# When three pieces of side work are handed out in a fused attention and gated-MLP kernel: the pause of a row-sum ring, one exponential, one total

## The chip, the cores and the metric

The kernel runs on one core of a Trainium2 chip. The metric is the device time of one execution in microseconds. Before the change it is 770.04 us (median of three runs, 769.9 to 770.56). The profiled execution has a span of 768.1 us and a mean granted TensorE clock of 0.999 of full speed, so the clock plays no part here.

The engines are named as follows. TensorE (PE) does the matmuls and PEld its weight loads; VectorE (DVE) and ScalarE (ACT) do the elementwise work; GpSimd (POOL) some sums and some transfers; SyncE (SP) issues most of the DMA transfers. Each engine works through its own queue in order, and waits for the others by semaphores.

## The reference

The sequence has 2048 rows of width 1024 in bf16. The first half is attention in which each position sees 8 positions, two apart, in 32 heads of 32; the second half is a gated MLP with 3584 hidden columns and no nonlinearity. Layernorm stands before both, and each half adds to its input.

```
def _A_ref(x, wqkv, wo):                      # H = 32, Dh = 32, W = 8, dil = 2
    qkv = (x @ wqkv).reshape(B, S, 3, H, Dh)  # then q, k, v as (B, H, S, Dh)
    idx = arange(S)[:, None] - (arange(W) * dil)[None, :]
    kg, vg = k[:, :, idx], v[:, :, idx]       # idx < 0 is masked
    logits = einsum("bhsd,bhswd->bhsw", q, kg) * Dh ** -0.5
    o = einsum("bhsw,bhswd->bhsd", softmax(logits), vg)
    return o.transpose(0, 2, 1, 3).reshape(B, S, D) @ wo

def _B_ref(x, w_gate, w_up, w_down):
    return ((x @ w_gate) * (x @ w_up)) @ w_down

h  = x + _A_ref(_layernorm(x), wqkv, wo)
h2 = h + _B_ref(_layernorm(h), w_gate, w_up, w_down)
```

## The kernel before

**Tiles and stages.** The rows go in four chunks of 512 (`TC`). A matmul has 128 x 128 weights and 512 moving columns, and fills one PSUM bank; a group of eight accumulates over the depth of 1024. All PSUM tiles come from one pool of eight banks. The stages in order of time, from the profile's chain of waits: the q, k, v projections to 188 us (with the output projection `wo` of chunk 0 from 155 to 169); the MLP's gate and up products of chunk 0 (`ffn1_first`, from 188 to 298, with `wo` of chunk 1 from 257 to 271); those of chunk 1 (`ffn1_second`, from 298 to 396); `wo` of chunk 2 (`wo_adds`); the down product of chunks 0 and 1 to 474; `wo` of chunk 3; the rest of that down product to 510; gate, up and down of chunks 2 and 3 to the end.

**Fewer products, scaled to f16.** Some of the large products are done as seven products of half size and not eight, on sums and differences of quarter matrices (`dprod` for the down product). For these, operands are turned into f16 with a power of two as scale, taken from the sum of absolute values. A `Scale` collects that: `add` sums the absolute values of a piece on ScalarE into one column of `l1` (L369, an activation with an accumulator, 1.90 us for 128 x 2048); `rows` adds up the columns on VectorE (L373, L374); `total` spreads the sum over the partitions by a matmul with ones (L379), and makes the factors from it on VectorE (L381 to L388). `scale_d` is that of `w_down`.

**The ring.** Of `w_down`, twelve pieces are summed when they are loaded for use (`abs_blocks`), and nine are loaded for their sum alone. That is `abs_down` (L678): one buffer of the weight pool (`wpool`, seven buffers) holds two pieces in turn, each loaded by a DMA that ScalarE issues (L688) and summed by ScalarE (L369). The summed piece is then overwritten by the load of the piece after next.

**The planner.** `Background` deals out side work between the matmul groups while the program is written. Each piece of side work is a Python generator. After every group, `bg.step(GROUP_US)` adds 1.73 us of credit and lets generators run up to their next `yield`; a number is the VectorE time to charge, and `("later", t)` says not to come back before t us of the planner's time. So a `yield` decides where in each engine's queue the next instructions stand, before the chip has seen anything. `abs_down` asks for `6.0 * GROUP_US` between pieces.

**Side work around the change.** Attention 2 and 3 are such generators: VectorE forms the logits (L546 to L556), takes their maximum off (L562 to L567), ScalarE does the exponential in two halves (L570), VectorE sums (L573) and multiplies with v (L594 on). So is `Norm2.finish`, the second layernorm of chunk 1 on ScalarE after `wo_1`: row sums and squares (L279, L637, L638), the normalized rows (L304), and their transposition by DMA (L632) for `ffn1_second`.

**Chunk 1 of the MLP.** `ffn1_second` runs seven blocks of four gate and four up groups. Each group gets a bank, and ScalarE casts it into one of three parts of a small ring in SBUF (L783). VectorE multiplies gate and up (L766), SyncE stores the product to `hd1` in DRAM (L769), and when that has landed the part of the ring can be written again. ScalarE also sums absolute values here, of the products and of weights (L369). SyncE's queue holds these stores and the loads of the weights (L172) in the order in which the planner met them; a load is put there when a buffer of the seven has been given back (`retire`, `pump`).

**The down product.** In the loop over q at L1228 VectorE converts `a21` and `a22` (L1084), with `scale_d.rows()` between them, and TensorE runs `scale_d.total` in the third round, ahead of the rest of that round's work. The factors from it release the conversions of the weights and their differences `t` (L1096), which TensorE takes from 447 us on.

Of the kernel before, what the change touches and what calls it, by code (L numbers as in the profile page):

```python
# [78 lines left out]
def kernel(  # L79
# [47 lines left out]
    def f16(ap):  # L127
        return ap.bitcast(F16)
# [37 lines left out]
    def pump(limit=None, wt=None):  # L166
        state["limit"] = limit or state["limit"]
        while state["next"] < state["limit"] and state["live"] < 7:
            key, src, n = stream[state["next"]]
            if wt is None:  # L170
                wt = wpool.tile([128, KO, 512], BF, tag="w", name="w_" + "_".join(map(str, key)))
            nc.sync.dma_start(wt[:, 0:n, :], src)  # L172
            wts[key] = wt
            wt = None
            state["next"] += 1
            state["live"] += 1

    def retire(n=1):
        state["live"] -= n
        pump()  # L180
# [22 lines left out]
    def load_x(c, what, eng, after=None):  # L203
        tiles = []
        for t in range(4):
            xt = hp.tile([128, D], BF, tag="h", name=f"{what}{c}_{t}")
            if after is not None and t == 0:
                nc.gpsimd.tensor_copy(xt[:, 0:1], after)
            eng.dma_start(xt[:], x[bass.ds(c * TC + t * 128, 128), :])
            tiles.append(xt)  # L210
        return tiles
# [275 lines left out]
    def mm_group(ps, wt, j, rhs):  # L487
        for ko in range(KO):
            nc.tensor.matmul(ps[:], lhsT=wt[:, ko, bass.ts(j, 128)], rhs=rhs[:, ko, :],  # L489
                             start=(ko == 0), stop=(ko == KO - 1))  # L490
# [44 lines left out]
    def attention(c):  # L535
# [29 lines left out]
        nc.vector.tensor_tensor(mx[:], tr[:, 0], tr[:, 1], ALU.max)  # L565
        for ws in (slice(0, 4), slice(4, 8)):
            nc.vector.tensor_tensor(lg[:, ws], lg[:, ws], mx[:, None, :].to_broadcast((128, W // 2, SUB)), ALU.subtract)  # L567
        yield "later", 4.0 if c == 0 else 1.5
        for ws in (slice(0, 4), slice(4, 8)):
            nc.scalar.activation(lg[:, ws], lg[:, ws], ACTF.Exp, scale=float(DH) ** -0.5)  # L570
        yield 3.5
# [99 lines left out]
    scale_gu, scale_d, scale_h = Scale("gu", 28), Scale("d", 21), Scale("h", 56)  # L671
    scale_h1 = Scale("h1", NF + NP)

    def abs_sum(key, c, b, i, junk):
        wt = wts[key, c, b]
        scale_gu.add((14 if key == "wu" else 0) + 2 * b + i, wt[:, bass.ts(i, 4), :], junk)

    def abs_down():  # L678
        ring = wpool.tile([128, KO, 512], BF, tag="w", name="w_ring")

        def rows_of(p):
            return ring[:, bass.ds(4 * (p % 2), pieces[p].shape[1]), :]

        pieces = [wd_v[:, bass.ts(p, 4), 512:1024] for p in range(7)]
        pieces += [wd_e[0][:, 0:4, 0:512], wd_e[0][:, 4:7, 0:512]]

        def load(p):
            nc.scalar.dma_start(rows_of(p), pieces[p])  # L688

        for p in range(2):  # L690
            load(p)
        yield "later", 12.0
        for p in range(9):
            scale_d.add(p, rows_of(p), rows_of(p))
            if p + 2 < 9:
                load(p + 2)
            yield "later", 6.0 * GROUP_US
        retire()

    def abs_blocks(tiles):  # L700
# [10 lines left out]
    def ffn1_first(lnT, at):  # L711
        hT, late = [], []
        junk = lnTp.tile([128, 4, 512], BF, tag="lnT", name="junk_g")

        def finish():
            gs, us = late.pop()
            nc.vector.tensor_tensor(gs[:], gs[:], us[:], ALU.mult)
            bg.spend(0.36)
            hT.append(gs)

        def sum_h(f):
            if f >= 0:
                scale_h1.add(f, hT[f][:], junk[:, 0, :])

        for b in range(7):
            if b == 2:
                hss[1] = load_x(1, "h", nc.sync)
            for j in range(4):
                if (b, j) in at:
                    at[b, j]()  # L730
                pg = psum.tile([128, TC], F32, tag="mm", name=f"pg0_{b}_{j}")
                mm_group(pg, wts["wg", 0, b], j, lnT)
                gs = t1k.tile([128, TC], BF, tag="t1k", name=f"gs0_{b}_{j}")
                nc.scalar.copy(gs[:], pg[:])
                if late:
                    finish()
                bg.step(GROUP_US)
                pu = psum.tile([128, TC], F32, tag="mm", name=f"pu0_{b}_{j}")
                mm_group(pu, wts["wu", 0, b], j, lnT)
                us = t1k.tile([128, TC], BF, tag="t1k", name=f"us0_{b}_{j}")  # L740
                nc.scalar.copy(us[:], pu[:])
                late.append((gs, us))
                if j % 2 and b not in (4, 5):
                    abs_sum("wg", 0, b, j // 2, junk[:])
                sum_h(len(hT) - 2)
                bg.step(GROUP_US)
            retire(2)
        finish()
        for f in range(NF - 3, NF):
            sum_h(f)  # L750
        return hT

    def ffn1_second(lnT, at):
        ring = [lnTp.tile([128, KO, TC], BF, tag="lnT", name=f"ring{i}") for i in range(2)]
        junk = ring[1][:, 4:8, :]
        late, done = [], []

        def sum_last():
            if done:
                i, g = done.pop()  # L760
                scale_h1.add(NF + i, g, junk[:, 0:2, :])

        def finish():
            i, g, u = late.pop(0)
            sum_last()
            nc.vector.tensor_tensor(g, g, u, ALU.mult)  # L766
            bg.spend(0.62)
            done.append((i, g))
            nc.sync.dma_start(hd1[:, bass.ts(i, 2), :], g)  # L769

        for b in range(7):
            if b == 5:
                hss[2] = load_x(2, "h", nc.sync)
            if b == 6:
                bg.spend(8.0)
            for j in range(4):
                i, k = divmod(4 * b + j, 2)
                part = ring[i % 3 // 2][:, bass.ts(i % 3 % 2, 4), :]
                g, u = part[:, 0:2, :], part[:, 2:4, :]
                for what, dst in (("wg", g), ("wu", u)):  # L780
                    ps = psum.tile([128, TC], F32, tag="mm", name=f"p{what}1_{b}_{j}")
                    mm_group(ps, wts[what, 1, b], j, lnT)
                    nc.scalar.copy(dst[:, k, :], ps[:])  # L783
                    if what == "wg" and late:
                        finish()
                    if what == "wu":
                        if k:
                            late.append((i, g, u))
                        if j % 2:
                            abs_sum("wu", 1, b, j // 2, junk)  # L790
                        elif b in (4, 5):
                            abs_sum("wg", 1, b, j // 2, junk)
                    bg.step(GROUP_US)
            retire(2)
            if b in at:
                at[b]()
        finish()
        sum_last()
# [275 lines left out]
    bg.add(sums, bg.now + 10.0, first=True)  # L1074
    hT0 = ffn1_first(lnT2_0, {(5, 0): wo_1})
    bg.finish(norm2[1])
    ffn1_second(norm2[0].lnT, {})
    bg.finish(sums)

    def to_f16(dst, src, sc, eng=nc.vector):  # L1080
        if eng is nc.scalar:
            nc.scalar.activation(dst, src, ACTF.Copy, scale=sc)
        else:
            eng.tensor_scalar(dst, src, sc, None, ALU.mult)  # L1084
# [56 lines left out]
    def cells_of(homes, n=8):  # L1141
        return [t[:, k, :] for t in homes for k in range(n)][0:NP]
# [55 lines left out]
    def s1_half(i):  # L1198
        n = (8, 6)[i]
        s, t = (f16(a[i][:, 0:n, :]) for a in (a21, a22))  # L1200
        nc.vector.tensor_tensor(s, s, t, ALU.add)

    def conv_h1(a, i, eng=nc.vector):
        n = (8, 6)[i]
        to_f16(f16(a[i][:, 0:n, :]), a[i][:, 0:n, :], scale_h1.s, eng)
# [22 lines left out]
    for q in range(4):  # L1228
        dprod(xs[q], q, A11, cells_of(b11, NH), True)
        if q == 0:  # L1230
            conv_h1(a21, 0)
            scale_d.rows()
            conv_h1(a22, 0)
        if q == 1:
            conv_h1(a21, 1, nc.scalar)
        if q == 2:
            scale_d.total(ys[3])
            inv1 = const.tile([128, 1], F32, name="inv_h1d")
            nc.vector.tensor_tensor(inv1[:], scale_h1.inv, scale_d.inv, ALU.mult)
            inv1 = inv1[:]  # L1240
            s1_half(0)
            for i in range(3):
                seed(i)
            conv_h1(a22, 1, nc.scalar)
# [28 lines left out]
    for q in range(4):  # L1273
        ev = psum.tile([128, TC], F32, tag="mm", name=f"ev{q}")
        dprod(ev, q, FS1, fcells(b11), True)
        p = lnp.tile([128, TC], F32, tag="ln", name=f"ep5_{q}")
# [173 lines left out]
    for q in range(4):  # L1450
        dprod(ps_x[q], q, S1, fcells(t1h), True)
        p = lnp.tile([128, TC], F32, tag="ln", name=f"dp5_{q}")
# [60 lines left out]
```

## Time and profile before

| | before |
|---|---|
| time, median of 3 | 770.04 us (769.9 to 770.56) |
| span of the profiled execution | 768.1 us |
| TensorE busy | 761.1 us, 99% |
| VectorE busy | 627.5 us, 82% |
| ScalarE busy | 533.0 us, 69% |
| DMA, mean rate | 190 GB/s |

The page gives the busy time of each engine. A wait is listed as the engine and line that waited, the engine and line that released it, the sum in us, how often, and the longest. A line of the timeline has the start, the length, the engine, the line of the kernel, the operation, out<-in, the shape and the count, and in brackets the idle time before it and who ended it. TensorE's lengths overlap, because matmuls are pipelined: the starts tell the pace. In a table by stage each engine's busy time is followed by its number of instructions, and the last three columns are the granted clock, the DMA share and GB/s.

Where the page puts ScalarE's work of interest: the nine sums of the ring start between 212.3 and 311.5 us; the normalized rows of chunk 1 (L304) at 282.97, 285.20, 287.90 and 291.96; the exponentials of attention 2 at 294.66 and of attention 3 at 384.03.

### The profile page before, as it was taken

The numbers are of one execution on the slowest core, as the hardware profiler recorded it, in microseconds if no ns is written. First come the engines' busy times: TensorE is split into PE (matmuls) and PEld (weight loads), VectorE is DVE, ScalarE is ACT, GpSimd is POOL, SyncE is SP. The second block draws the span as 40 slices with busy tenths as digits, with TensorE's granted clock in tenths as the row PEclk, the third lists the DMA queues.
The fourth block names the chain that finished last, engine by engine and source line by source line (L and its number), as shares of the span: only waits on it lengthen the run. The fifth ranks groups of instructions, "written<-read, shape, count | busy, mean of one in ns | idle before, by whom it ended". The sixth has DMA issues, their size and how long they took to land.

```text
span 768.1 us, 10356 instructions
## 1 busy us (share of the span) xinstructions
PE 761.1 (99%) x3648; PEld 349.3 (45%) x3648; DVE 627.5 (82%) x760; ACT 533.0 (69%) x1012; POOL 144.5 (19%) x155
## 2 busy tenths in 40 slices
PE   8999999999999999999999999999999999999998
PEld 6444444444444444444444444444444444444444
DVE  6789999999999998999999999976554444578862
ACT  4756854556799599975899985846777677788230
POOL 0010000200001000001000002008778777600000
PEclk9999999999999999999999999999999999999999
DMA  8899794967998959779679438684242423830001
GB/s 273 224 236 261 187 285 117 308 180 192 328 347 283 301 193 312 242 248 310 199 242 301 154 109 268 152 201 131 72 109 56 111 81 84 263 121 27 1 28 55
DMA packets 191987, 145.77 MB, mean 190 GB/s; under 512 B 81856, under 2 KB 182080, under 8 KB 189888
## 3 DMA queue, kind: packets, MB, share of 16 engines
q1 hardware_dynamic: 180416, 116.94, 53.5%
q0 software_dynamic: 3728, 22.02, 8.4%
q10 hardware_dynamic: 7792, 6.16, 2.7%
q8 instruction: 28, 0.46, 0.3%
q14 instruction: 23, 0.19, 0.1%
HBM read 111.02 MB, written 27.26 MB: 180 GB/s over the span
## 4 chain that ended last, share of the span: by engine, by line
PE 75%; DVE 14%; ACT 5%; issue 2%; DMA 2%; SPq 0%; ACTq 0%; DVEq 0%
PE ps L489 17%; PE dx L1103 6%; PE pz L843 6%; PE px L843 6%; PE py L843 6%; PE pg L489 6%; PE pu L489 5%; PE wo L661 4%; PE ez L1103 3%; PE pv L843 3%; PE ey L1103 3%; PE dy L1103 3%; DVE prod L546 2%; PE wo L1157 2%; DVE pv L594 2%
## 5 line engine op out<-in xcount | busy, mean ns | idle before, releaser
L489 PE MATMUL ps<-lnT,w_qkv 128*128 128x512 bf16 x608 | 132.1, 379 | 0.0
L489 PEld LDWEIGHTS <-w_qkv 128*128 128x128 bf16 (+1 forms) x608 | 59.3, 98 | 70.9
L546 DVE TENSOR_TENSOR prod<-qD,kD 128x4096 bf16<-128x4096 bf16 (+1 forms) x34 | 72.3, 2158 | 2.9 <-DMA kD<-kd 2.9
L594 DVE TENSOR_TENSOR pv<-vD,at 128x4096 bf16<-128x4096 bf16 x32 | 72.4, 2285 | 0.3
L489 PEld LDWEIGHTS <-w_wg 128*128 128x128 bf16 x448 | 43.8, 98 | 54.1 <-issue 1.3
L843 PEld LDWEIGHTS <-sw 128*128 128x128 f16 x448 | 43.8, 98 | 52.9 <-issue 0.2
L489 PEld LDWEIGHTS <-w_wu 128*128 128x128 bf16 x448 | 43.8, 98 | 52.9
L403 ACT CAST sg<-ps 128x512 bf16<-128x512 f32 x72 | 41.6, 584 | 31.1 <-PE ps L489 26.6
L843 PE MATMUL px<-lnT,ws 128*128 128x512 bf16 x224 | 55.2, 379 | 0.0
L489 PE MATMUL pwg<-lnT,w_wg 128*128 128x512 bf16 x224 | 52.9, 379 | 1.0 <-ACT ring L783 1.0
L489 PE MATMUL pu<-lnT,w_wu 128*128 128x512 bf16 x224 | 52.9, 379 | 0.0
L489 PE MATMUL pg<-lnT,w_wg 128*128 128x512 bf16 x224 | 52.9, 379 | 0.0
L489 PE MATMUL pwu<-lnT,w_wu 128*128 128x512 bf16 x224 | 52.9, 379 | 0.0
L843 PEld LDWEIGHTS <-ws 128*128 128x128 f16 x336 | 32.9, 98 | 39.6
L607 POOL DMA_DIRECT2D od<-oD x4 | 2.2, 542 | 253.3 <-DVE oD L605 253.3
L824 POOL TENSOR_TENSOR sw<-ws 128x512 f16<-128x512 f16 x26 | 30.0, 1153 | 78.8 <-ACT pz L868 47.1
L1103 PEld LDWEIGHTS <-gs 128*128 128x128 f16 (+1 forms) x280 | 27.2, 98 | 34.3 <-issue 1.3
L548 DVE TENSOR_TENSOR prod<-prod 128x4096 bf16<-128x4096 bf16 x16 | 36.6, 2287 | 0.3
L860 ACT COPY py<-px 128x512 f32<-128x512 f32 x28 | 16.0, 570 | 24.5 <-PE px L843 24.5
L827 POOL TENSOR_TENSOR sw<-ws,sw 128x512 f16<-128x512 f16 x26 | 30.6, 1175 | 0.0
L825 POOL TENSOR_TENSOR sw<-sw,ws 128x512 f16<-128x512 f16 x26 | 30.0, 1154 | 2.0
L826 POOL TENSOR_TENSOR sw<-ws 128x512 f16<-128x512 f16 x26 | 30.2, 1161 | 0.0
(371 smaller groups left out, 1577.5 us busy)
## 6 DMA issues: line engine op xcount, KB each, us to landing
w_wg<-in_B_w_gate_dram SPq DMA_DIRECT2D x14, 1024.0 KB, 7.9
w_wu<-in_B_w_up_dram SPq DMA_DIRECT2D x14, 1024.0 KB, 7.7
w_pair<-in_B_w_gate_dram SPq DMA_DIRECT2D x14, 512.0 KB, 4.0
w_pair<-in_B_w_up_dram SPq DMA_DIRECT2D x14, 512.0 KB, 5.3
w_wo<-in_A_wo_dram SPq DMA_DIRECT2D x6, 1024.0 KB, 8.3
w_qkv<-in_A_wqkv_dram SPq DMA_DIRECT2D x5, 1024.0 KB, 9.2
kd<-sg SPq DMA_DIRECT2D x32, 144.0 KB, 4.2
vd<-sg SPq DMA_DIRECT2D x32, 144.0 KB, 3.4
```

The source lines that it names most:

```text
L403: nc.scalar.copy(sg[:, HB:HB + TC], ps[:])
L489: nc.tensor.matmul(ps[:], lhsT=wt[:, ko, bass.ts(j, 128)], rhs=rhs[:, ko, :], start=(ko == 0), stop=(ko == KO - 1))
L546: nc.vector.tensor_tensor(prod[:, j, ds], qD[:, ds], kD[:, ds, o:o + SUB], ALU.mult)
L548: nc.vector.tensor_tensor(prod[:, :, 0:16], prod[:, :, 0:16], prod[:, :, 16:32], ALU.add)
L594: nc.vector.tensor_tensor(pv[:, j], vD[:, :, o:o + SUB], at[:, w, None, :].to_broadcast((128, DH, SUB)), ALU.mult)
L661: nc.tensor.matmul(ps[:], lhsT=oTs[c][:, kk, t, :], rhs=wts["wo", c, hf][:, kk, :], start=(kk == 0), stop=(kk == KO - 1))
L824: eng.tensor_tensor(sw[:, i, 0], a21, a22, ALU.add)
L825: eng.tensor_tensor(sw[:, i, 1], sw[:, i, 0], a11, ALU.subtract)
L826: eng.tensor_tensor(sw[:, i, 2], a11, a21, ALU.subtract)
L827: eng.tensor_tensor(sw[:, i, 3], a12, sw[:, i, 1], ALU.subtract)
L843: nc.tensor.matmul(ps[:], lhsT=lhs[:, ko, :], rhs=rhs[:, ko, :], start=(fresh and ko == 0), stop=(ko == 3), skip_group_check=not fresh)
L1103: nc.tensor.matmul(ps[:, bass.ds(lo, n)], lhsT=lhs[k][:, bass.ts(q, 128)], rhs=rhs[k][:, bass.ds(lo, n)], start=(fresh and k == 0), stop=( ...
```

## The change

Three edits of order. No instruction is added or dropped on any engine, apart from the places where they stand.

1. `abs_down` stops after its fifth piece (p == 4) until the second layernorm of chunk 1 has been written out (`normed`), and goes on in chunk 1. It is meant to leave ScalarE to the layernorm and to attention 2's exponential.
2. Attention 3 hands out its exponential 3.0 us and not 1.5 us of planner's time after its logits: one group later. It is meant to let one more cast go ahead of it.
3. `scale_d.rows()` goes ahead of the conversion of `a21`, so that the total's matmul has its operand earlier.

On ScalarE's queue the first edit moves pieces 5 to 8 of the ring. They stood in chunk 0's blocks 5 and 6 and at the first group of chunk 1; now they stand after the first up group of chunk 1's block 0, after that block's weight sum, in the middle of block 1 and in the middle of block 2. The buffer of the ring is given back later. In SyncE's queue the gate weights of chunk 1's blocks 4, 5 and 6 therefore each move behind the one or two ring stores that followed them. The second edit swaps the two exponentials with one cast (L783, block 5, j 1, gate). The third swaps VectorE's L373 and L374 with one L1084. TensorE's and GpSimd's orders are unchanged.

```diff
@@ attention(c)
-        yield "later", 4.0 if c == 0 else 1.5
+        yield "later", {0: 4.0, 3: 3.0}.get(c, 1.5)
         for ws in (slice(0, 4), slice(4, 8)):
             nc.scalar.activation(lg[:, ws], lg[:, ws], ACTF.Exp, scale=float(DH) ** -0.5)
@@ before abs_down
+    normed = set()
@@ abs_down
             if p + 2 < 9:
                 load(p + 2)
             yield "later", 6.0 * GROUP_US
+            while p == 4 and 1 not in normed:
+                yield "later", 1.0
         retire()
@@ main order
     hT0 = ffn1_first(lnT2_0, {(5, 0): wo_1})
     bg.finish(norm2[1])
+    normed.add(1)
     ffn1_second(norm2[0].lnT, {})
@@ down product, for q in range(4)
         dprod(xs[q], q, A11, cells_of(b11, NH), True)
         if q == 0:
+            scale_d.rows()
             conv_h1(a21, 0)
-            scale_d.rows()
             conv_h1(a22, 0)
```

## The prediction

> **What bounds the kernel now.** I read the page's busy shares first, then who waits for whom on TensorE, then the timelines around each of its waits. TensorE is at work almost throughout, and it waited only three times for as much as 0.3 us after the start-up:
>
> ```profile
> PE 761.1 (99%) x3648; PEld 349.3 (45%) x3648; DVE 627.5 (82%) x760; ACT 533.0 (69%) x1012; POOL 144.5 (19%) x155
> ```
> ```profile
> PE pwg L489 <- ACT ring L783: 1.0, 1, 1.0
> ...
> PE ey L379 <- DVE rowbd L374: 0.3, 1, 0.3
> PE ey L1103 <- DVE t L1096: 0.3, 1, 0.3
> ```
>
> Busy time of pipelined matmuls flatters, so I took start to start: consecutive 512-column matmuls start 0.216 us apart (a group of eight takes 1.73 us), and anything beyond is lost. After the first 20 us the start times show eight such gaps of 0.06 us or more: 1.20 us at 384.6, 0.45 at 419.2, 0.10 at 447.1, 0.43 at 448.7, and 0.12, 0.20, 0.08 and 0.25 at 462, 498, 514 and 717. Their sum, 2.83 us, is all that a change of order can save; more than that would need fewer matmuls.
>
> The largest gap, TensorE's timeline and then ScalarE's:
>
> ```profile
> 381.13 1.89 PE L489 MATMUL pwg<-lnT,w_wg 128*128 128x512 bf16 x8
> 382.86 1.89 PE L489 MATMUL pwu<-lnT,w_wu 128*128 128x512 bf16 x8
> 385.79 1.89 PE L489 MATMUL pwg<-lnT,w_wg 128*128 128x512 bf16 x8 [1.04 <-ACT ring L783]
> ```
> ```profile
> 378.22 1.98 ACT L369 ACTIVATE ring<-w_wg 128x2048 bf16<-128x2048 bf16 x1
> 380.03 0.26 ACT L369 ACTIVATION_READ_ACCUMULATOR ring<-w_wg 128x1 f32 x1
> 384.03 1.23 ACT L570 ACTIVATE lg<-lg 128x512 f32<-128x512 f32 x2 [3.74 <-DVE lg L567]
> 385.17 0.57 ACT L783 CAST ring<-pwg 128x512 bf16<-128x512 f32 x1
> 385.64 0.59 ACT L783 CAST ring<-pwu 128x512 bf16<-128x512 f32 x1
> ```
>
> The reader should see ScalarE's queue stopped for 3.74 us at attention 3's exponential, for logits that VectorE has not finished. The cast behind it is of group (block 5, j 1, gate), whose matmuls ended at 372.5. All eight banks are full, so TensorE stands until that cast returns one. ScalarE was late already: 5.21 us at 362.75 for a store of the ring that landed late, behind weight loads.
>
> VectorE is the next limit. In the table by stage (TensorE, its weight loads, VectorE, ScalarE, GpSimd) it has 13.8 to 13.9 us of every 14 from 298 to 382, of which these two rows are the first:
>
> ```profile
> 298.00:312.00 14.00, 14.00 (x66) 6.37 (x65) 13.92 (x11) 13.12 (x25) 0.00 (x0) 1.00 1.04 316
> 312.00:326.00 14.00, 14.00 (x67) 6.36 (x65) 13.91 (x8) 14.00 (x24) 0.00 (x0) 1.00 0.65 203
> ```
>
> It lost time just before, to a late ScalarE:
>
> ```profile
> 293.71 0.42 DVE L717 TENSOR_TENSOR gs<-gs,us 128x512 bf16<-128x512 bf16 x1 [1.09 <-ACT us L741]
> 295.86 0.69 DVE L573 TENSOR_TENSOR trs<-lg 128x512 f32<-128x512 f32 x1 [1.72 <-ACT lg L570]
> ```
>
> And the second gap, VectorE's order, then TensorE's:
>
> ```profile
> 418.08 1.28 DVE L1084 TENSOR_SCALAR a<-a,sbh 128x4096 f16<-128x4096 bf16 x1
> 419.27 0.17 DVE L373 TENSOR_REDUCE rowd<-l1d 128x1 f32<-128x21 f32 x1
> 419.48 0.16 DVE L374 CAST rowbd<-rowd 128x1 bf16<-128x1 f32 x1
> ```
> ```profile
> 419.69 0.38 PE L379 MATMUL ey<-rowbd,ones 128*128 128x512 bf16 x1 [0.28 <-DVE rowbd L374]
> ```
>
> TensorE was ready at 419.24; the total had to wait for a conversion that nobody needed yet.
>
> **What the Trainium skill says.** "TensorE: Matmul & The Clock Gate", Back-to-back issue gap and the lines before it, gives 216 ns between 512-column matmuls; this trace has 0.216. "PSUM — Partial Sum Buffer", Specifications (TRN2), gives 8 banks, each for one 512-column fp32 output; the trace agrees, as TensorE stopped when the group eight back was not yet cast. "ScalarE: Activation LUTs", What ACT_TABLE_LOAD costs, prices an ACTIVATE with immediates at 186 ns + 0.833 ns a column, 1.89 us for 2048; the ring sums here took 1.90. "DMA: Bandwidth & Descriptors", Queues, rings and completion order, has the issues of one queue on one set of rings, each consumed in order, so that a small store stands behind earlier loads; here the store issued at 352.98, after two 1 MB loads at 345.2 and 345.7, landed only at 362.7.
>
> **Part 1, the ring's pause.** Comparing the order of instructions on each engine, pieces 5 to 8 of the w_down row sum leave ScalarE's queue at 272.07, 289.04, 300.45 and 311.46 and come back between 311 and 338, one each at about block 0 start, block 0 end, block 1 middle, block 2 middle of chunk 1. Each costs 1.90 us (the last 1.49), and where it issues a load 0.5 more with the semaphore; nothing is added or removed.
> Gain: at 272 ScalarE can instead take the third row tile as soon as VectorE's addition ends (272.8), so 274.51 becomes about 272.9: 1.6 us. Piece 6 gives 2.4 more. Attention 2's exponential at 294.66 could then start at 290.7, but its logits end at 292.62 less the 0.82 us that VectorE no longer waits at 280.70: 291.8. So the sums at 295.86 start at about 293.2, and VectorE is 2.66 us ahead. Since it has next to no idle time from 298 to 384, it keeps that.
> Cost: ScalarE's backlog was 10.5 us at 310.5 (the cast of a group whose matmuls ended at 299.98). VectorE's lead shrinks it to 7.9; the four pieces then add 0.9, 2.4, 1.9 and 1.5, against casts and sums that leave ScalarE 2.7 us idle per 14 after 326. I get backlogs of 6.4 at block 1 and about 4 at block 2. TensorE stops only when a backlog passes about 11.5 us (seven groups of 1.73 less the cast): nothing on the path. The ring's buffer is held some 27 us longer, so chunk 1's gate weights of blocks 4, 5 and 6 are issued behind one or two ring stores: at about 330, 342 and 351, needed at 353, 367 and 381. With 8 us to land, hidden. The new order also puts the store at 352.98 ahead of one of the two loads, so the 5.21 us wait at 362.75 should be nearly gone.
>
> **Part 2, the exponential a group later.** One cast now goes ahead of the two activations. The cast of 385.17 runs at about 380 and the bank is free 5 us sooner; the next cast (385.64) inherits the wait. Its bank is needed 1.73 us later, at 386.3, and it ends by 385.8: the 1.20 us are saved even with everything else late, and with part 1's 2.7 us there is slack. VectorE's sums behind the exponential still follow VectorE's own logits at once. Cost nothing, as ScalarE was idle 3.74 us there.
>
> **Part 3, the total first.** The reduce and its cast (0.4 us with their semaphores) pass ahead of a 1.2 us conversion. The last partial sum's accumulator is read at 418.2, so they could end at 418.6, 0.6 us before TensorE comes: 0.45 us saved. Behind them the two conversions start 0.4 us later or less; VectorE's own reading of the total follows TensorE's matmul.
>
> **The later gaps.** The total then lets VectorE go on at about 418.7 and not 420.76, so 2.0 us earlier; TensorE comes 1.75 us earlier to the t factors (1.20 + 0.45 + 0.10). Of the 0.43 us, 0.43 − (2.0 − 1.75) = 0.18 stay. The four small gaps stay; they follow VectorE. Sum: 1.20 + 0.45 + 0.10 + 0.25 = 2.0 us, and 770.04 − 2.0 = 768.0.
>
> **Rivals.**
> A, only the bank gap goes: VectorE does not keep its lead (a ring store or a late cast takes it), and TensorE meets the same waits for the total or the t factors again. 770.04 − 1.2 = 768.8. For it: VectorE is 99% busy from 412 to 440 and 95% from there to 474, so any delay there returns. Against: the order is the same and no wait on it gets later.
> B, no stall is left: 770.04 − 2.83 = 767.2. For it: VectorE 2 us earlier might cover the small gaps too. Against: TensorE gets just as much earlier.
> C, slower: the ring's sums in chunk 1 meet an undiminished backlog. 10.5 + 2.4 + 2.4 = 15.3 us is 3.8 over the 11.5 that eight banks hold, less the 0.45 of part 3: 773.4. For it: ScalarE was 14.0 us busy of 14 from 312 to 326. Against: the same work has left the stretch before.
> D, the stalls move and cancel, say a bank wait of 1 to 2 us at 386 to 390, as ScalarE's casts of block 5 run 11 to 12.5 us late in the trace of before: 769.8.
>
> **How the numbers follow.** Forecast 0.50, A 0.20, B 0.13, D 0.07, C 0.10. The time is 768.0. The range from 766.9 (B and the spread of the runs) to 769.8 (D) leaves out C and a little. Faster by over 0.2% is below 768.5: the forecast and B, 0.62 with a little off for their edges and from A; the same, A and D, 0.27; slower 0.11.
>
> **What would show it.** Right: no TensorE wait for ACT L783 near 384, none for rowbd; the wait before the trs sums at 295 below 1.1 us; ScalarE's wait for a ring store near 362 under 1 us; the first cast of chunk 1 near 308; total span about 766. Wrong: a TensorE wait for a bank between 310 and 345 (C) or at 386 to 390 (D), a wait for w_wg in blocks 4 to 6, or VectorE at the t factors no earlier than before (A).

## Result and profile after

The changed kernel takes 767.78 us (median of six runs, 767.47 to 768.34) against 770.07 for the kernel before on the same chip: 2.3 us less, ratio 0.997 with a 95% interval of 0.9957 to 0.9982. The forecast was 768.0.

The page's busy times and the list of what TensorE waited for:

```profile
PE 757.3 (99%) x3592; PEld 349.5 (46%) x3648; DVE 627.1 (82%) x760; ACT 532.7 (70%) x1012; POOL 144.7 (19%) x155
```
```profile
PE warm_ps L357 <- DVE warm L343: 1.2, 1, 1.2
PE ez L1108 <- DVE hsr L805: 0.5, 1, 0.5
PE ps L450 <- ACT lnT L445: 0.5, 1, 0.5
```

VectorE and ScalarE do the same work as before, to 0.4 us. None of the three waits that the prediction showed is left: no ring (the bank), no rowbd, no t. Two of the lines belong to the start-up; one, for hsr near 496 us, is new as an entry (the prediction counted it as a gap of 0.20 us at 498). 56 matmul records are missing (3592 of 3648), so TensorE's busy time can't be compared; all 3648 weight loads are there, and their starts are what I compare below.

This profile is 0.49 us ahead of the one before already at 10 us, where both kernels issue the same instructions. A second profile of the changed kernel (the run e8_changed_again below) begins within 0.04 us of the kernel before, so the times below are read from that one where nothing else is said. VectorE:

```profile
290.38 1.29 DVE L567 TENSOR_TENSOR lg<-lg,mx 128x512 f32<-128x512 f32 x2
291.59 0.42 DVE L721 TENSOR_TENSOR gs<-gs,us 128x512 bf16<-128x512 bf16 x1
292.37 0.69 DVE L573 TENSOR_TENSOR trs<-lg 128x512 f32<-128x512 f32 x1 [0.36 <-ACT lg L570]
...
381.81 0.69 DVE L573 TENSOR_TENSOR trs<-lg 128x512 f32<-128x512 f32 x1 [0.69 <-ACT lg L570]
...
414.47 0.16 DVE L374 CAST rowbd<-rowd 128x1 bf16<-128x1 f32 x1
414.56 2.48 DVE L1089 TENSOR_SCALAR a<-a,sbh 128x4096 f16<-128x4096 bf16 x2
418.42 0.16 DVE L381 COPY totd<-ey 128x1 f32<-128x1 f32 x1 [1.38 <-PE ey L379]
...
442.80 3.95 DVE L1101 TENSOR_TENSOR t<-b,w_dn 128x3584 f16<-128x3584 f16 x2
```

Two of the same instructions in the kernel before:

```profile
385.30 0.69 DVE L573 TENSOR_TENSOR trs<-lg 128x512 f32<-128x512 f32 x1 [0.69 <-ACT lg L570]
...
445.13 3.94 DVE L1096 TENSOR_TENSOR t<-b,w_dn 128x3584 f16<-128x3584 f16 x2
```

Attention 2's sums start at 292.37 and not 295.86: VectorE is 3.49 us ahead. At attention 3's sums (381.81 against 385.30) it is still 3.49 us ahead, so ninety microseconds of nearly full VectorE carry the lead unchanged. The total's operand is ready at 414.6, and now VectorE waits 1.38 us for TensorE's matmul. At the t factors it is 2.33 us ahead (442.80 against 445.13).

ScalarE and TensorE in the same profile:

```profile
307.02 0.57 ACT L787 CAST ring<-pwg 128x512 bf16<-128x512 f32 x1
...
359.74 0.59 ACT L787 CAST ring<-pwg 128x512 bf16<-128x512 f32 x1 [3.58 <-DMA hd<-ring]
...
377.11 0.64 ACT L787 CAST ring<-pwg 128x512 bf16<-128x512 f32 x1
380.55 1.23 ACT L570 ACTIVATE lg<-lg 128x512 f32<-128x512 f32 x2 [2.80 <-DVE lg L567]
381.69 0.57 ACT L787 CAST ring<-pwu 128x512 bf16<-128x512 f32 x1
```
```profile
384.55 1.67 PE L489 MATMUL pwg<-lnT,w_wg 128*128 128x512 bf16 x7
386.27 1.89 PE L489 MATMUL pwu<-lnT,w_wu 128*128 128x512 bf16 x8
...
418.00 0.38 PE L379 MATMUL ey<-rowbd,ones 128*128 128x512 bf16 x1
```

The group that started at 385.79 now starts at 384.55, and the next 1.72 us behind it, without a bracket. The cast of the second bank is 3.95 us earlier (381.69 against 385.64).

The starts of the 3648 weight loads, each against the same load of the kernel before, give the account:

| at us (of before) | gap before | won |
|---|---|---|
| 385.8, bank | 1.20 | 1.20 |
| 419.7, total | 0.45 | 0.44 |
| 447.2 and 449.1, t | 0.53 | 0.52 |
| 462 | 0.12 | 0.10 |
| 498, 514, 717 | 0.53 | 0.03, at 498 |

The last load starts 2.35 us earlier, of which 0.04 is start-up: 2.31 us, and the times show 2.3. The sum holds for this profile only. In the first one the 0.49 us of start-up are not kept: TensorE loses 0.47 us more at 498, and its last load is 2.31 us earlier with the start-up counted in. What decides there is in "The wait that is left" below.

How far ScalarE's cast of a group starts behind the end of its matmuls, both profiles (chunk 1 of the MLP, first gate group of a block, and its largest; block 3, where it is at most about 4 us, is left out):

| block | before | after | largest before | largest after |
|---|---|---|---|---|
| 0 | 10.5 | 7.0 | 10.5 | 7.0 |
| 1 | 5.8 | 5.8 | 5.8 | 5.8 |
| 2 | 3.4 | 3.6 | 3.7 | 3.6 |
| 4 | 7.5 | 4.5 | 8.0 | 5.0 |
| 5 | 7.2 | 4.2 | 12.7 | 8.5 |
| 6 | 11.9 | 7.9 | 11.9 | 7.9 |

By the prediction's estimate eight banks stand about 11.5 us. After the change no cast comes near that. Where the ring's pieces were put (blocks 0 to 2), the lag is larger than before by more than 0.2 us only in the last groups of blocks 1 and 2, by up to 2 us (4.2 against 2.3 in one of them): elsewhere VectorE's lead outweighs the added pieces.

### The profile page after: what moved, and what is told of

Read it like the earlier page. It is cut to its first block, busy times and chain, and to the rows that moved or that the text cites. A ratio compares the mean times of both kernels' runs of the same rounds, so it can differ in the third digit from the quotient of the medians.

```text
span 765.8 us, 10299 instructions
## 1 busy us (share of the span) xinstructions
PE 757.3 (99%) x3592; PEld 349.5 (46%) x3648; DVE 627.1 (82%) x760; ACT 532.7 (70%) x1012; POOL 144.7 (19%) x155
## 4 chain that ended last, share of the span: by engine, by line
PE 69%; DVE 20%; ACT 6%; issue 3%; DMA 2%; SPq 0%; DVEq 0%; ACTq 0%
PE ps L489 16%; PE dx L1108 6%; PE pz L847 6%; PE pwu L489 6%; PE py L847 6%; PE px L847 6%; PE pwg L489 6%; PE pv L847 3%; PE dy L1108 3%; DVE pv L594 3%; DVE prod L546 3%; DVE prod L548 2%; PE wo L1162 2%; DMA b21r<-in_B_w_down_dram 2%; PE ez L1108 2%
## 5 line engine op out<-in xcount | busy, mean ns | idle before, releaser
L847 PE MATMUL px<-lnT,ws 128*128 128x512 bf16 x212 | 53.1, 379 | 0.6
```

The lines of the kernel that those rows point to most:

```text
L847: nc.tensor.matmul(ps[:], lhsT=lhs[:, ko, :], rhs=rhs[:, ko, :], start=(fresh and ko == 0), stop=(ko == 3), skip_group_check=not fresh)
```

## Experiments

Two theories. **The lead**: each of TensorE's stalls from 384 us on ended on VectorE's order of work, directly (rowbd, t) or through ScalarE (the exponential with the casts behind it); the pause puts VectorE 3 us ahead, and that alone lets all of them go. **Each edit its own stall**, as the prediction had it: 1.20 us is part 2's and 0.45 part 3's. Times in one paragraph are from one chip, beside the kernel before on it.

**The pause alone.** The kernel before with the first edit only.

```diff
+    normed = set()
...
+            while p == 4 and 1 not in normed:
+                yield "later", 1.0
...
+    normed.add(1)
```

> Part 1 alone, the ring's pause, with attention 3's exponential and the total where they were before. Theory 1 (the lead): what pays is that VectorE is some 3 us ahead from attention 2's exponential on, and this lead covers all the later gaps on TensorE; so part 1 alone gives all or nearly all of the change, 1.6 to 2.3 us less than before (767.8 to 768.5), no TensorE wait near 384, none for the total's operand, none for the t factors. Theory 2 (each edit its own gap): part 2 owns the 1.20 us at 384 and part 3 the 0.45 us at 419, so part 1 alone gives only the rest, about 0.5 us (769.6), and both those gaps are still there.

Measured: 767.92 us (767.41 to 768.38) beside 770.18; ratio 0.9969, 0.9958 to 0.9981. That is 2.26 us, all but the whole. ScalarE near 380, and the only entry of TensorE's waits that is not of the start-up:

```profile
380.38 1.23 ACT L570 ACTIVATE lg<-lg 128x512 f32<-128x512 f32 x2 [3.93 <-DVE lg L567]
381.51 0.57 ACT L787 CAST ring<-pwg 128x512 bf16<-128x512 f32 x1
```
```profile
PE ez L1108 <- DVE hsr L805: 0.3, 1, 0.3
```

ScalarE still stands 3.93 us ahead of the exponential, and the cast that part 2 would pass ahead still stands behind it. It does not matter, because all of it happens 3.66 us earlier (381.51 against 385.17; 0.2 of it is start-up). The total's operand, still behind a conversion, is ready near 415.9 for a TensorE that comes at 417.8.

**The other two edits, each alone and together.**

```diff
-        yield "later", 4.0 if c == 0 else 1.5
+        yield "later", {0: 4.0, 3: 3.0}.get(c, 1.5)
```
```diff
         if q == 0:
+            scale_d.rows()
             conv_h1(a21, 0)
-            scale_d.rows()
```

> Part 2 alone, attention 3's exponential one group later. Theory 1: the bank gap of 1.20 us at 384 goes, but VectorE is no earlier than about 0.5 us (the last casts of chunk 1 come one cast sooner), so TensorE reaches the total and the t factors sooner and waits there for what it has gained: 0 to 0.6 us less than before (769.5 to 770.1), the gap at 419 near 1.2 us. Theory 2: 1.2 us less (768.9), the gap at 419 still 0.45.

> Part 3 alone, the row total ahead of the conversion. Theory 1: the gap of 0.45 us at 419 goes, but VectorE's own work between there and the t factors is the same and no earlier, so the gap at the t factors (0.43) grows by the same 0.45: no change, 770.1 within 0.2. Theory 2: 0.45 us less (769.6).

> Parts 2 and 3 without the pause. Theory 1: both their gaps go, and the t factors' gap takes nearly all of it, as VectorE is at most 0.5 us earlier: 0 to 0.6 us less than before (769.5 to 770.1), with a wait of 1.0 to 1.7 us at the t factors near 447. Theory 2: 1.65 us less (768.4).

Measured: the exponential alone 769.77, ratio 0.9997 (0.9989 to 1.0006); the total alone 770.36, 1.0001 (0.9993 to 1.001); both 769.93, 0.9996 (0.9988 to 1.0004), beside 770.18. None can be told from no change, as the first theory has it (the total alone is 0.06 us above its range); the second needed 768.9, 769.6 and 768.4. Two details of the first theory are missed. With the exponential alone the gap at 419 is 0.60 us and not 1.2, because 0.60 us have been lost again by 393; and with both edits the waits at t are 0.85 us and not 1.0 or more. TensorE with both:

```profile
391.62 1.89 PE L489 MATMUL pwg<-lnT,w_wg 128*128 128x512 bf16 x8 [0.29 <-ACT ring L783]
...
446.39 1.67 PE L1103 MATMUL ey<-t,gs 128*128 128x512 f16 x7 [0.58 <-DVE t L1096]
448.33 1.89 PE L1103 MATMUL ey<-t,gs 128*128 128x512 f16 x8 [0.27 <-DVE t L1096]
```

This is where the 1.20 and 0.45 us go. The bank wait at 384.6 is gone, and the weight loads have won 1.20 us; by 393 they have given back 0.60, in waits for the banks of the groups behind. Those lagged 12.1 to 12.5 us before, over what eight banks hold: the stall at 384.6 had hidden them. The total's 0.45 us is won as meant, and lost at t, where the two waits are 0.58 and 0.27; of these the kernel before has only the second. At 497 us 0.32 of what was won is left, and at 498 TensorE waits 0.6 us for hsr. The last weight load is 0.24 us ahead of the kernel before, and the profile was 0.48 ahead at 10 us already: nothing is left. With the total alone it is the same: won at 419, then 0.52 and 0.26 us at t, and 0.8 for hsr. The exponential alone still has 0.47 us at 497 in its trace, which the times can't tell from nothing.

**A lead made in another way.** The pause could also work because ScalarE itself is relieved. In the kernel before, one addition of attention 3 is left out (2.28 us of VectorE at 353), and nothing else is touched: the order on every engine is that of the kernel before.

```diff
-            nc.vector.tensor_tensor(prod[:, :, 0:16], prod[:, :, 0:16], prod[:, :, 16:32], ALU.add)
+            if (c, wp) != (3, 1):
+                nc.vector.tensor_tensor(prod[:, :, 0:16], prod[:, :, 0:16], prod[:, :, 16:32], ALU.add)
```

> The kernel before, with one addition of attention 3 left out (the upper half of the products of the second pair of positions is not added; the output is not the reference's). VectorE is 2.29 us ahead from 353 us on, and no order changes. The first theory (a lead of VectorE is enough, whatever makes it): the bank wait near 384 falls from 1.04 us to under 0.2, rowbd is not waited for, 768.0 to 768.8. Its rival, the pause matters because ScalarE itself has less to do before 311: ScalarE as late as before, the bank wait stays at 0.8 us or more, 769.6 to 770.1.

Measured: 767.95 (767.42 to 768.58) beside 770.35; ratio 0.9967, 0.9955 to 0.998, just under the first theory's range. ScalarE near 380 and TensorE:

```profile
381.23 1.23 ACT L571 ACTIVATE lg<-lg 128x512 f32<-128x512 f32 x2 [1.53 <-DVE lg L568]
382.37 0.57 ACT L784 CAST ring<-pwg 128x512 bf16<-128x512 f32 x1
```
```profile
384.10 1.67 PE L489 MATMUL pwg<-lnT,w_wg 128*128 128x512 bf16 x7
385.83 1.89 PE L489 MATMUL pwu<-lnT,w_wu 128*128 128x512 bf16 x8
```

ScalarE is as it was until then: its ring store is still waited for 5.1 us, and the sums at 295 still wait 1.72. VectorE's lead is enough, and the bank, total and t waits are all gone. Up to 497 us the weight loads win 2.29 us, as in the changed kernel. This shows the mechanism without any of the three edits.

**Part of the lead given back.** The changed kernel with one product of attention 3 formed twice (2.2 us more of VectorE).

```diff
-                    nc.vector.tensor_tensor(prod[:, j, ds], qD[:, ds], kD[:, ds, o:o + SUB], ALU.mult)
+                    for _ in range(2 if (c, wp, j) == (3, 1, 0) else 1):
+                        nc.vector.tensor_tensor(prod[:, j, ds], qD[:, ds], kD[:, ds, o:o + SUB], ALU.mult)
```

> The changed kernel with one VectorE multiplication of 2.2 us done twice in attention 3's logits (the same product written a second time, nothing left out). Theory 1: of VectorE's lead of about 3.4 us over the kernel before, 2.2 are gone; VectorE reaches the total's result about 1 us after it is there, and the t factors come 0.8 to 1.1 us late, so the time is 0.7 to 1.2 us above the changed kernel's 767.8: 768.5 to 769.0, with a wait of TensorE for the t factors near 446. Theory 2 (the gain is ScalarE's own, banks freed in time): VectorE has room, no change, 767.8.

Measured: 768.38 (767.93 to 768.92) beside 770.25; ratio 0.9974, 0.9965 to 0.9984. Just under the first theory's range, 0.6 over the 767.78 measured for the changed kernel beside another series of the kernel before. Attention 3's sums start at 383.89, a lead of 1.4 us (0.3 of it start-up), and of the three waits one is back, at t:

```profile
447.39 4.91 PE L1109 MATMUL ey<-t,gs 128*128 128x512 f16 x22 [0.27 <-DVE t L1102]
```

The lead pays first for the bank and the total, and what remains of it for t. The times overlap with the changed kernel's, so the row is the firmer evidence; up to 497 us the weight loads win 1.46 us and not 2.29.

**The ring's buffer held, without the pause.** A third theory: the gain is in SyncE's queue, where the pause moves chunk 1's gate weights behind ring stores. Here the buffer is only given back later, which makes SyncE's order that of the changed kernel and moves nothing else.

```diff
             yield "later", 6.0 * GROUP_US
+        yield "later", 33.0
         retire()
```

> Nothing of the change but its order on SyncE's queue: the ring's pieces stay where they were before, and only its buffer is given back later, so that the gate weights of blocks 4, 5 and 6 stand behind the ring stores as in the changed kernel. Theory 1 (VectorE's lead pays): ScalarE's 5.2 us wait near 362 for a ring store shrinks below 3 us, its casts run less late, but attention 3's exponential still stands ahead of the cast and waits for the same late logits, and VectorE is no earlier: 0 to 0.3 us less than before (769.8 to 770.1). Theory 3 (the earlier landing of the stores pays): ScalarE keeps up, the bank gap of 1.20 us goes and most of the change is here: 768.0 to 768.9.

Measured: 770.35 beside 770.25; ratio 1.0001, 0.9993 to 1.0009. ScalarE's wait and TensorE's:

```profile
ACT ring L784 <- DMA hd<-ring: 5.2, 1, 5.2
```
```profile
PE pwg L489 <- ACT ring L784: 1.1, 1, 1.1
```

There is no gain, so the third theory falls; the first was nearer, if 0.25 us too hopeful. The wait for the store, which was to fall below 3 us, is what it was.

**The wait that is left.** At 498 us TensorE waits for VectorE's `hsr` (L805), which stands behind two conversions of 2 us, `t_half`. VectorE comes to these after a row statistic, which stands on ScalarE behind a scaling of rows and the conversion of the weights `b21`; and that conversion waits for their load. The kernel before, then the first profile of the changed kernel:

```profile
481.26 6.46 ACT L1082 ACTIVATE b21r<-b21r,sbd 128x3584 f16<-128x3584 bf16 x2 [4.68 <-DMA b21r<-in_B_w_down_dram]
```
```profile
478.95 6.46 ACT L1087 ACTIVATE b21r<-b21r,sbd 128x3584 f16<-128x3584 bf16 x2 [5.15 <-DMA b21r<-in_B_w_down_dram]
```

How many us each profile is ahead of that of the kernel before (TensorE by its weight loads):

| run | TensorE at 10 us | TensorE at 497 us | start of b21's conversion | TensorE's last load |
|---|---|---|---|---|
| changed, first profile | 0.49 | 2.78 | 2.30 | 2.31 |
| changed, second (e8) | 0.04 | 2.33 | 2.35 | 2.35 |
| pause alone (e1) | 0.21 | 2.50 | 2.22 | 2.23 |
| less work before (e10) | 0.49 | 2.77 | 2.25 | 2.25 |
| lead given back (e6) | 0.29 | 1.75 | 1.52 | 1.52 |
| exponential alone (e2) | 0.14 | 0.60 | 0.76 | 0.76 |
| total alone (e3) | 0.07 | -0.08 | -0.81 | -0.81 |
| exponential and total (e4) | 0.48 | 0.80 | 0.24 | 0.24 |
| ring held (e5) | 0.06 | 0.02 | -0.29 | -0.30 |

The last two columns agree within 0.01 us in every row. In these profiles the landing of b21 sets the pace from 498 us on, and what TensorE has won by 497 beyond it is lost, start-up included; where b21 is further ahead (e2), the wait at 498 shrinks. The load is issued earlier where VectorE is ahead, but takes 12.0 to 13.0 us until its conversion starts; why it varies is not shown. The edits themselves are better compared up to 497 us (third column less second): 2.29 us for the changed kernel in both profiles and for less work before, 2.30 for the pause alone, 1.46 with part of the lead given back.

One of the two conversions of 2 us can come a little later, which takes it out of the chain from the load to `hsr`.

```diff
-    t_half(t4, b21, t2, 1)
     for q in range(4):
         dprod(zs[q], q, F11, fcells(b12), False)
...
         put(1, q, 1, hsr1[:, q, 512:1024], zs[q], inv1, p5t[q][:])
+        if q == 0:
+            t_half(t4, b21, t2, 1)
```

> The changed kernel, with the second of the two last differences (t4) behind the first result of the ez bank on VectorE and not ahead of it. In the changed kernel TensorE's only wait over 0.3 us after the start is 0.66 us near 495, for that result, which stands behind both differences of 2.0 us each. If VectorE's order is what it waits for, the wait goes, as the first result is 2 us earlier and the second difference still comes in time for the eighth matmul: 0.4 to 0.7 us less than the changed kernel, 767.1 to 767.4. If it is ScalarE's conversion behind the late load of b21, as the chain says, the first difference is as late as before and the wait stays at 0.3 us or more: 767.5 to 767.8.

Measured: 767.67 (767.43 to 767.84) beside 770.25, ratio 0.9965, 0.9952 to 0.9977. The wait went; the time is that of the theory in which it stays. The 0.66 us that I meant to save were those of the first profile, start-up included: against the second, which starts alike (0.04 us at 10, here 0.07), the last load is only about 0.2 us earlier. A last comparison took the changed kernel again, and this edit on the pause alone:

> The changed kernel once more, beside the next two on one chip. 767.5 to 768.1 us as before, ratio 0.997. It is the yardstick for the pause with the later t4.

> The ring's pause alone (the second and third edit undone), and t_half(t4, b21, t2, 1) moved behind the first put of the products zs with F22. The first theory (the pause makes the lead and the other two edits return nothing): no TensorE wait for ACT L787, rowbd or t, none of 0.3 us for hsr at 498; 767.4 to 767.9, not above the changed kernel. The second theory (the other two edits own 1.2 and 0.45 us): 769.0 or more.

Measured: the changed kernel 768.02 (767.91 to 768.05), the pause with the later t_half 767.39 (767.28 to 767.68), beside 770.35; ratios 0.9968 (0.9956 to 0.9981) and 0.9961 (0.9947 to 0.9974). No run of one reaches the other. TensorE of the latter:

```profile
495.38 5.99 PE L1108 MATMUL ez<-t,a22r 128*128 128x512 f16 x27
```

Its weight loads win 0.20 us at 498. The other 0.3 us between the two profiles stands at 10 us already, in the start-up. So 0.2 of the 0.63 us between the medians is traced to the edit. A part of the rest may be start-up that only the kernel without the wait keeps: here 0.37 us are kept to the end, while the first profile of the changed kernel lost 0.47 of its 0.49 at 498. Whether the executions without a trace differ in this way is not shown. The kernel with the lowest median of the study thus has one of the three edits and one that the change did not have; with all three and the later `t_half` it is 767.67, on another chip, and the two overlap.

## Why the prediction was right, and which steps failed

**The bound and the total: right.** Eight gaps, 2.83 us in sum, were all that could be won; 2.31 were in the second profile, and 2.0 was forecast. The result lies between the forecast (768.0) and rival B (767.2). The gaps were counted from a pace of 0.216 us, and it holds: from 200 to 380 us all matmuls of the kernel before start 0.215 to 0.216 us apart. The section of the Trainium skill that the prediction cites for it ("TensorE: Matmul & The Clock Gate", Back-to-back issue gap) also has about 131 ns for a stream of weight loads and matmuls of 512 columns; this trace does not agree with that, and the measurement decides.

**Part 1, VectorE's lead: right in kind, too small.** 2.66 us was forecast, 3.49 measured. The logits end 0.95 earlier (0.82 forecast). The rest is the exponential: I let the sums wait until both halves of the logits were done. ScalarE takes the first half as soon as VectorE has subtracted its maximum, at 291.11, so the sums start 1.99 us behind the subtraction's start and not the 2.7 I reckoned with. The wait at the sums was to fall below 1.1 us; it fell to 0.36. That the lead is kept to 384 held exactly.

**Part 1, ScalarE's backlog: right.** Forecast 7.9 at the first group of chunk 1, 6.4 in block 1, about 4 in block 2; measured 7.0, 5.8 and at most 3.6. Rival C needed over 11.5. The table by stage of the changed kernel's first profile shows what made C plausible: ScalarE (fourth busy time) fills the stretch with the last ring piece, and TensorE loses nothing there.

```profile
326.00:340.00 14.00, 13.95 (x65) 6.34 (x65) 13.93 (x9) 14.00 (x24) 0.54 (x1) 1.00 0.76 262
```

**Part 1, the ring store: wrong.** "The 5.21 us wait at 362.75 should be nearly gone", under 1 us; it is 2.8 us in one profile and 3.58 in the other. I had taken from the Trainium skill ("DMA: Bandwidth & Descriptors", Queues, rings and completion order) that a small store stands behind earlier loads of its queue, and then counted one load fewer ahead of it. SyncE's rows with the buffer held show the slip: one weight load moves behind that store, but the gate weights of the block before move down into its place, so two loads are still ahead (344.82 and 345.63, the store at 352.96). The wait is then 5.2 us, as before. No run contradicts the page; I misapplied it. In the changed kernel the store is issued 3.5 us earlier and still takes some 10 us to land (359.7); ScalarE only comes 1.4 us earlier itself, and so waits less. No time hung on it.

**Part 2: wrong as a part of its own.** "The 1.20 us are saved even with everything else late." With everything else late, 0.60 of it was lost again within 8 us and 0.15 more at the total; with part 3 beside it, the rest went at t and 498. I looked at one bank behind the exponential; rival D had named the casts of block 5 that lag 11 to 12.5 us, and without the pause that is what happens. With the pause the swap has nothing left to save.

**Part 3: wrong as a part of its own.** The 0.45 us at 419 is won, and lost at t. The step behind it, "the total then lets VectorE go on at about 418.7 and not 420.76", fails: reading the total (L381) stands behind both conversions in VectorE's queue, so passing the total ahead of one moves it not at all. With part 3 alone it was read at 420.84. What brought it to 418.42 in the changed kernel is the lead.

**The later gaps: the size failed.** Of the 0.43 us, 0.18 was to stay; none did. VectorE is 2.33 us ahead at t and not 2.0, TensorE 1.64 to 1.74, and the difference of 0.6 covers the gap. "The four small gaps stay; they follow VectorE": three stayed (498, 514, 717), the one at 462 went. The one at 498 does not follow VectorE alone, but the landing of b21, which the prediction left out: from 497 us to the end that gave back 0.16 us in e2 and took 0.74 in e3.

So the total was right partly by compensation: 1.20 and 0.45 were put to the edits that stood beside them, while the first edit, to which I gave no TensorE time directly, was worth all of it: up to 497 us TensorE wins 2.30 us with the pause alone and 2.29 with all three edits, so parts 2 and 3 add nothing to it there. The times say the same within their spread: 2.26 us without them, 2.29 and 2.33 with them, each against its own series of the kernel before. That these end so near the 2.29 is in part luck as well: the landing of b21 happened to be 2.2 to 2.35 us earlier.

## What to carry to other kernels

When several stalls of the bounding engine end on the same other engine, ask how late that engine is and where it fell behind: here one idle stretch taken from it ahead of a long full stretch was worth more than a local swap at each stall. A swap at one stall has to be followed to the next wait on the same engine, since the bounding engine then comes earlier to a partner who does not. And a list of lags (cast against its matmuls) showed stalls that a larger one hid, which the list of waits did not. Last, follow a gain to the end of the program: here it passes a load whose landing decides anew how much of it is kept.

## What the runs showed that I had not expected

Profiles with the same instructions differ by up to 0.5 us in the first 10 us, while the x rows and the first weights arrive, and by under 0.1 us from there to 384 us. A difference between two spans below that says nothing unless the start is taken out, and that is right only up to the next wait that does not move with the start: at 498 us the first profile of the changed kernel lost 0.47 of its 0.49 us.

The load of b21 takes 12.0 to 13.0 us from its issue to the start of its conversion over the twelve profiles. Where the conversions of 2 us stand as they did, the end of the kernel follows it within 0.01 us.
